# The rows of the large tiles in another order in DRAM: a grouped-query attention decode step with a gated MLP on one Trainium2 core

## The chip, the core and the metric

The kernel runs on one core of a Trainium2 chip. A core has five engines: TensorE (PE, with its weight loads, PEld), VectorE (DVE), ScalarE (ACT), GpSimd (POOL) and SyncE (SP), which here only issues transfers. Sixteen DMA engines move data between DRAM (HBM) and SBUF, the core's working memory of 128 partitions. The metric is the device time of one execution in microseconds; lower is better. Times of several executions are given as their median.

## The reference

One decode step for a batch of 8: a layer norm of x, attention over a cache of 4096 positions (32 query heads, 8 heads of K and V, head size 128), and a gMLP branch on x that gates the result. Everything is float32.

```python
def _A_ref(x, k_cache, v_cache, wq, wo):          # x is the layer-normed input, [8, 1, 512]
    q = (x @ wq).reshape(B, Sq, Hq, Dh).transpose(0, 2, 1, 3)
    k = jnp.repeat(k_cache, rep, axis=1)          # k_cache, v_cache: [8, 8, 4096, 128]
    v = jnp.repeat(v_cache, rep, axis=1)
    scores = jnp.einsum("bhqd,bhkd->bhqk", q, k) * (Dh ** -0.5)
    p = _softmax(scores, axis=-1)
    o = jnp.einsum("bhqk,bhkd->bhqd", p, v)
    return o.transpose(0, 2, 1, 3).reshape(B, Sq, Hq * Dh) @ wo

def _B_ref(x, w_in, w_sp, b_sp, w_out):
    z = _gelu(jnp.einsum("bsd,df->bsf", x, w_in))
    z1, z2 = z[..., :Fh], _layernorm(z[..., Fh:], axis=-1)
    g = jnp.einsum("ts,bsf->btf", w_sp, z2) + b_sp[None, :, None]
    return jnp.einsum("bsf,fd->bsd", z1 * g, w_out)

s = _A_ref(_layernorm(x), A_k_cache, A_v_cache, A_wq, A_wo)
g = _silu(_B_ref(x, B_w_in, B_w_sp, B_b_sp, B_w_out))
return x + s * g
```

Two things make up nearly all of the bytes: K and V, 134 MB each. Every byte of them is read once.

## The kernel before

SBUF holds three large buffers, the slots A, B and C, each 128 partitions of 16384 floats (64 KB a partition, 8 MB a slot). Everything large passes through them. `wq` goes to B and the weights of the MLP (`w_mlp`, 10496 floats a partition) to C; a small remainder of the MLP's output weights, `w_ext`, goes to the end of 32 partitions of C. Then for each of the eight K/V heads four loads follow: K for the first half of the batch to A (`load_k`, L591), K for the second half to B, V for the first half to C (`load_v`, L596), V for the second half to B again. At the end `wo` goes to A in seven pieces (`load_wo`, L601), of 14 down to 1 of its 32 blocks of 512 floats. In the last head the second half of V comes as two loads (L596 and L597).

All of these loads are issued by SP, one after the other, in the order in which they stand in the code. A load into a slot waits until PE has made the last matmul on what the slot held; the next load in SP's order cannot be issued before it. There are 42 loads of large tiles, one of `w_ext`, and the store of the result. The two loads of x are issued by ACT.

For a head, PE multiplies the query, spread over 32 columns, with K (L550, `scores`), DVE and ACT make the softmax, PE turns the probabilities round (L572) and multiplies them with V (L582, `values`), DVE picks and adds what belongs together (L584, L585), and PE folds the result (L588). The loop over heads is one on PE and DVE. A recording layer (`Recorder`) notes every operation with its reads and writes, derives the waits from them, and then writes the program out engine by engine; it does not reorder anything.

On the host, `kernel` lays every large array out so that DRAM holds the tile as it is to stand in SBUF: a row per partition, 128 rows for each load, and row p of DRAM goes to partition p. For K and V the arrays have the shape heads x 2 halves x 128 x 16384; `wq` and `wo` are 128 x 16384, `w_mlp` is 128 x 10496. A load of a slot thus reads 8 MB that lie in DRAM in one piece. For `wo` and for the split load of V a part of each row is read.

`w_ext` is the exception. In DRAM it has 8 groups of 4 rows and an unread fifth row, and the load reads groups and rows as two dimensions (L371).

Of the kernel before, what the change touches and what calls it, by code (L numbers as in the profile page):

```python
# [15 lines left out]
P = 128  # L16
B, D = 8, 512
# [23 lines left out]
XK = XG * XR  # L41
XC = P // XK
LAST = NB - 1


class Region:
# [300 lines left out]
def gqa_gmlp_decode(real, x, kT, v, wq, wo, w_mlp, w_ext, out):  # L347
    nc = Recorder(real)

    def sb(name, shape, **kw):  # L350
        return real.alloc_sbuf_tensor(name, shape, F32, **kw).ap()
# [4 lines left out]
    slots = {n: sb(f"slot_{n}", [P, SLOT], align_bytes=ALIGN) for n in "ABC"}  # L356
# [5 lines left out]
        nc.scalar.dma_start(xs_sb[:, c:c + XW // X_PARTS], x[:, c:c + XW // X_PARTS])  # L362
    x_sb = xs_sb[:, :D]

    nc.sync.dma_start(slots["B"], wq, key="B")
    wq_sb = slots["B"].rearrange("p (k n) -> p k n", k=NK)
    n_in, n_mlp = NK * 2 * FH, NK * 2 * FH + NB * D - XN
    nc.sync.dma_start(slots["C"][:, :n_mlp], w_mlp, key="C")
    w_in_sb = slots["C"][:, :n_in].rearrange("p (k n) -> p k n", k=NK)
    ext = slots["C"][:XK, n_mlp:n_mlp + XC * XN]  # L370
    nc.sync.dma_start(ext, w_ext[:, :XR])  # L371
# [59 lines left out]
    for i in range(E):  # L431
        for g in range(G):
            lo = g * P + i * W
# [23 lines left out]
    def mlp():  # L457
# [45 lines left out]
        nc.vector.tensor_copy(hT.rearrange("p a s -> p (a s)"), th)  # L503
        low = R * (LAST // 2)
        hX = tbuf[:XK, 2 * P + D:2 * P + D + XC * R].rearrange("p (c r) -> p c r", r=R)
        tx = scr[2][:XK, :XC * R].rearrange("p (c r) -> p c r", r=R)
        for c in range(XC):
            lo = (LAST % 2) * P + c * XK
            nc.tensor.transpose(tx[:, c, :], u[low:low + R, 1, lo:lo + XK], ident[low:low + R, low:low + R])
        nc.vector.tensor_copy(hX, tx)  # L510
        for j in range(NB):
            g = j % G
            w_j = w_out_sb(j)
            nc.tensor.matmul(sc[R * g:R * (g + 1), 0, :w_j.shape[1]], hT[:, j % 2, R * (j // 2):R * (j // 2 + 1)],
                             w_j, start=(j < G), stop=(j + G >= NB and j < LAST))
        g = LAST % G
        for c in range(XC):
# [70 lines left out]
        nc.tensor.matmul(po[:, b * REP:(b + 1) * REP], o_sb[b % 2], fold, start=True, stop=True)  # L588

    def load_k(h, half, n):  # L590
        nc.sync.dma_start(slots[n], kT[h, half], key=n)  # L591
        return slots[n].rearrange("p (i c g s) -> p i c g s", i=HALF, c=2, g=G)

    def load_v(h, half, n, own=0):
        cut = SLOT * (HALF - own) // HALF
        nc.sync.dma_start(slots[n][:, :cut], v[h, half][:, :cut], key=n)  # L596
        rest = nc.sync.dma_start(slots[n][:, cut:], v[h, half][:, cut:]) if own else None  # L597
        return slots[n].rearrange("p (i j e) -> p i j e", i=HALF, j=J), rest

    def load_wo(lo, hi):  # L600
        nc.sync.dma_start(slots["A"][:, lo * D:hi * D], wo[:, lo * D:hi * D])  # L601

    wo_sb = slots["A"].rearrange("p (m d) -> p m d", d=D)
    part, acc = sc[:, 0, :], sc[:, 1, :W]
# [16 lines left out]
    def head(h):  # L621
        spread_q(h)
        for half, n in enumerate("AB"):
            scores(half, load_k(h, half, n))
        softmax()
        for half, n in enumerate("CB"):
            v_sb, rest = load_v(h, half, n, 1 if h == HKV - 1 and half else 0)
            for i in range(HALF):
                b = half * HALF + i
                values(b, v_sb[:, i], rest if b == B - 3 else None)  # L630
                if b > 0:
                    combine(b - 1)
        combine(B - 1)
        if h < FOLDED // REP:
            to = oT[:, h]
        else:
            m = h * REP - FOLDED
            to = oT_end[:, m:m + REP, (E - 1) * B:E * B]
        nc.stored = nc.scalar.activation(to, po.rearrange("p (b r) -> p r b", r=REP), AF.Copy)
# [9 lines left out]
    for lo, hi in WO_PIECES:  # L649
        load_wo(lo, hi)  # L650
# [4 lines left out]
    for i in range(E):  # L655
        for g in range(G):
            lo = g * P + i * W
# [45 lines left out]
```

## Time and profile before

| | |
|---|---|
| time, median of 3 runs | 678.54 us (678.11 to 678.82) |
| span of the profiled execution, first to last instruction | 677.4 us |
| PE busy | 377.2 us (56%) |
| DVE busy | 165.3 us (24%) |
| ACT, POOL busy | 15.0 us (2%), 4.4 us (1%) |
| read from HBM, over the span | 290.74 MB, 429 GB/s |
| chain that ended last | DMA of wo 7%, PE L550 1%, the rest under 0.5% each |

The profile is of one execution. Its span runs from the first instruction to the last, and the time of an execution has a little more around it: the median lies 1.1 us above the span. The page gives busy time by engine, the span in 40 slices with the busy share in tenths, the share of the DMA engines and what they moved, and the chain of work that ended last, followed back from the last instruction. It reaches back only to the loads of wo, which were issued at 627 to 630 us and then waited behind earlier loads. For what comes before, the DMA rows of the slices have to be read, and SP's waits.

### The profile page before, as it was taken

The numbers are of one execution on the slowest core, as the hardware profiler recorded it, in microseconds if no ns is written. First come the engines' busy times: TensorE is split into PE (matmuls) and PEld (weight loads), VectorE is DVE, ScalarE is ACT, GpSimd is POOL, SyncE is SP. The second block draws the span as 40 slices with busy tenths as digits, with TensorE's granted clock in tenths as the row PEclk, the third lists the DMA queues.
The fourth block names the chain that finished last, engine by engine and source line by source line (L and its number), as shares of the span: only waits on it lengthen the run. The fifth ranks groups of instructions, "written<-read, shape, count | busy, mean of one in ns | idle before, by whom it ended". The sixth has DMA issues, their size and how long they took to land. (4 is left out here: it accounts for less than half of the span.)

```text
span 677.4 us, 6190 instructions
## 1 busy us (share of the span) xinstructions
PE 377.2 (56%) x2670; PEld 120.7 (18%) x2670; DVE 165.3 (24%) x262; ACT 15.0 (2%) x35; POOL 4.4 (1%) x22
## 2 busy tenths in 40 slices
PE   0638654546765464555755355656745356655576
PEld 0122121112211121111211021111211021111222
DVE  2051042301430033401521024400422024400442
ACT  0000000000000000000000000000000000000000
POOL 1000000000000000000000000000000000000000
PEclk9986767888776567878767678876667788876679
DMA  8999999999999999999999999999999999999997
GB/s 373 441 442 431 433 434 433 434 433 433 433 433 438 433 433 433 433 433 433 437 433 433 433 441 433 433 433 437 437 437 433 433 433 433 433 433 437 423 424 305
DMA packets 6270, 290.86 MB, mean 429 GB/s; under 512 B 840, under 2 KB 856, under 8 KB 1528
## 3 DMA queue, kind: packets, MB, share of 16 engines
q1 hardware_dynamic: 6232, 290.75, 99.2%
q8 instruction: 5, 0.08, 0.0%
q10 hardware_dynamic: 32, 0.02, 0.0%
q14 instruction: 1, 0.01, 0.0%
HBM read 290.74 MB, written 0.03 MB: 429 GB/s over the span
## 5 line engine op out<-in xcount | busy, mean ns | idle before, releaser
L550 PE MATMUL sc<-slot_B,qz 128*32 128x512 f32 x512 | 74.3, 745 | 77.9 <-PEq L550 77.9
L582 PE MATMUL o_ps<-slot_B,tbuf 128*16 128x512 f32 x512 | 76.9, 728 | 63.8 <-PEq L582 63.8
L550 PE MATMUL sc<-slot_A,qz 128*32 128x512 f32 x512 | 72.8, 733 | 44.9 <-PEq L550 44.9
L582 PE MATMUL o_ps<-slot_C,tbuf 128*16 128x512 f32 x512 | 76.8, 741 | 13.6 <-PEq L582 12.7
L584 DVE TENSOR_TENSOR o_all<-o_ps,diag 128x512 f32<-128x512 f32 x64 | 44.3, 691 | 137.4 <-DVEq L584 137.4
L554 DVE TENSOR_REDUCE nm<-sc 128x1 f32<-128x1024 f32 x8 | 9.8, 1224 | 273.9 <-DVEq L554 273.9
L585 DVE TENSOR_REDUCE o_sb<-o_all 128x128 f32<-128x512 f32 x64 | 67.7, 1059 | 9.3
L550 PEld LDWEIGHTS sc<-slot_B,qz 128*32 128x32 f32 x512 | 20.3, 133 | 131.8 <-issue 131.8
L550 PEld LDWEIGHTS sc<-slot_A,qz 128*32 128x32 f32 x512 | 20.0, 132 | 91.2 <-issue 91.2
L588 PE MATMUL po<-fold,o_sb 128*128 128x4 f32 x128 | 24.4, 261 | 18.2 <-PEq L588 16.7
L588 PEld LDWEIGHTS po<-fold,o_sb 128*128 128x128 f32 x128 | 20.1, 198 | 74.3 <-issue 74.3
L582 PEld LDWEIGHTS o_ps<-slot_B,tbuf 128*16 128x16 f32 x512 | 13.5, 106 | 92.7 <-issue 92.2
L582 PEld LDWEIGHTS o_ps<-slot_C,tbuf 128*16 128x16 f32 x512 | 15.6, 112 | 55.7 <-issue 55.4
L572 PE MATMUL scr<-ident,pbuf 128*128 128x128 f32 x64 | 15.5, 423 | 13.4 <-PEq L572 13.4
L555 ACT ACTIVATE pbuf<-sc,nm 128x1024 f32<-128x1024 f32 x8 | 8.9, 1114 | 281.3 <-DVEq L554 281.3
L572 PEld LDWEIGHTS scr<-ident,pbuf 128*128 128x128 f32 x64 | 12.6, 223 | 13.8 <-issue 13.8
L447 PE MATMUL scr<-slot_B,xnT 128*32 128x512 f32 x64 | 9.8, 764 | 8.1 <-PEq L447 8.1
L573 DVE COPY tbuf<-scr 128x512 f32<-128x512 f32 x16 | 11.1, 692 | 12.4 <-DVEq L573 12.4
L558 PE MATMUL scr<-ident,nm 128*1 128x128 f32 x8 | 2.2, 269 | 13.6 <-PEq L558 13.6
L565 PE MATMUL scr<-wl,same 128*128 128x1 f32 x16 | 3.6, 297 | 8.0 <-PEq L565 8.0
L426 PE MATMUL scr<-ident,tbuf 8*128 8x8 f32 x4 | 0.6, 255 | 12.9 <-DVE tbuf L423 12.9
L609 PE MATMUL sc<-slot_A,oT 128*8 128x512 f32 x48 | 6.5, 593 | 0.9 <-DMA slot_A<-in_wo 0.9
(105 smaller groups left out, 84.0 us busy)
## 6 DMA issues: line engine op xcount, KB each, us to landing
slot_B<-in_v SPq DMA_DIRECT2D x1, 6144.0 KB, 25.8
slot_C<-in_w_mlp SPq DMA_DIRECT2D x1, 5248.0 KB, 33.7
slot_A<-in_wo SPq DMA_DIRECT2D x1, 3584.0 KB, 36.8
slot_B<-in_v SPq DMA_DIRECT2D x1, 2048.0 KB, 28.7
slot_A<-in_wo SPq DMA_DIRECT2D x1, 2048.0 KB, 41.2
slot_A<-in_wo SPq DMA_DIRECT2D x2, 768.0 KB, 43.3
slot_A<-in_wo SPq DMA_DIRECT2D x1, 512.0 KB, 44.7
slot_A<-in_wo SPq DMA_DIRECT2D x2, 256.0 KB, 45.0
```

The costliest lines, as they stand in the source:

```text
L447: nc.tensor.matmul(pq[R * g:R * (g + 1), :], xnT[:, k, :], wq_sb[:, k, lo:lo + REP * DH], start=(k == 0), stop=(k == NK - 1))
L550: nc.tensor.matmul(sc[R * g:R * (g + 1), c, :], qz[:, b * R:(b + 1) * R], k_sb[:, i, c, g, :], start=(b == 0), stop=(b == B - 1))
L554: nc.vector.tensor_reduce(nm, sc, op=ALU.max, axis=AX.XY, negate=True)
L555: nc.scalar.activation(p.rearrange("p j s -> p (j s)"), sc.rearrange("p c s -> p (c s)"), AF.Exp, bias=nm, accum_out=l)
L565: nc.tensor.matmul(tot, same_all, wl, start=True, stop=True)
L572: nc.tensor.transpose(t[:, j * P:(j + 1) * P], p[:, 4 * c + j, :], ident)
L573: nc.vector.tensor_copy(pT[:, :, 4 * c:4 * c + 4].rearrange("p b j (g r) -> p (j g) b r", g=G), t.rearrange("p (m b r) -> p m b r", b=B, r ...
L582: nc.tensor.matmul(of[R * c:R * c + G * REP, :], pT[:, b, j, :], v_unit[:, j], start=(j < G), stop=(j >= J - G))
L584: nc.vector.tensor_mul(o_all[b % 2], o, diag[:, :, None].to_broadcast([P, G, DH]), after=after)
L585: nc.vector.tensor_reduce(o_sb[b % 2], o_all[b % 2].rearrange("p g d -> p d g"), op=ALU.add, axis=AX.X)
L588: nc.tensor.matmul(po[:, b * REP:(b + 1) * REP], o_sb[b % 2], fold, start=True, stop=True)
L609: nc.tensor.matmul(part[R * r:R * r + B, :], oT[:, h, r, :], wo_sb[:, m, :], start=(m < REP), stop=(m >= FOLDED - REP))
```

## The change

In DRAM the 128 rows of every large tile are put in another order. The 128 partitions are seen as 16 groups (e) of 8 partitions (j). Before, the row of partition 8 e + j was row 8 e + j. Now it is row 16 j + e: first the first partition of each of the 16 groups, then the second of each, and so on. The host puts the arrays into this order, and each load names its DRAM rows as two dimensions, e outside and j inside (`by_engine`), so that every partition gets the data that it had before. `w_ext`, x and the store of the result stay as they are.

```diff
 LAST = NB - 1
+QUEUES = 16
+
+
+def by_engine(rows):
+    return rows.rearrange("(j e) n -> e j n", e=QUEUES)
...
-    nc.sync.dma_start(slots["B"], wq, key="B")
+    nc.sync.dma_start(slots["B"], by_engine(wq), key="B")
...
-    nc.sync.dma_start(slots["C"][:, :n_mlp], w_mlp, key="C")
+    nc.sync.dma_start(slots["C"][:, :n_mlp], by_engine(w_mlp), key="C")
...
     def load_k(h, half, n):
-        nc.sync.dma_start(slots[n], kT[h, half], key=n)
+        nc.sync.dma_start(slots[n], by_engine(kT[h, half]), key=n)
...
     def load_v(h, half, n, own=0):
         cut = SLOT * (HALF - own) // HALF
-        nc.sync.dma_start(slots[n][:, :cut], v[h, half][:, :cut], key=n)
-        rest = nc.sync.dma_start(slots[n][:, cut:], v[h, half][:, cut:]) if own else None
+        nc.sync.dma_start(slots[n][:, :cut], by_engine(v[h, half][:, :cut]), key=n)
+        rest = nc.sync.dma_start(slots[n][:, cut:], by_engine(v[h, half][:, cut:])) if own else None
...
     def load_wo(lo, hi):
-        nc.sync.dma_start(slots["A"][:, lo * D:hi * D], wo[:, lo * D:hi * D])
+        nc.sync.dma_start(slots["A"][:, lo * D:hi * D], by_engine(wo[:, lo * D:hi * D]))
...
+    for name in ("kT", "v", "wq", "wo", "w_mlp"):
+        a = arrays[name]
+        rows = a.reshape(a.shape[:-2] + (QUEUES, P // QUEUES, a.shape[-1]))
+        arrays[name] = c(rows.swapaxes(-3, -2)).reshape(a.shape)
```

The instructions of every engine stand in the same order as before, with the same waits. SP's loads alone have another form. The first of them before, each with the partitions and floats that it writes:

```order
L365 DMA slot_B<-in_wq 128x16384
L368 DMA slot_C<-in_w_mlp 128x10496
L371 DMA slot_C<-in_w_ext 32x1x1024
L591 DMA slot_A<-in_kT 128x16384
L591 DMA slot_B<-in_kT 128x16384
L596 DMA slot_C<-in_v 128x16384
L596 DMA slot_B<-in_v 128x16384
```

And the same place in the changed kernel, whose lines stand five lower:

```order
L370 DMA slot_B<-in_wq 128x1x16384
L373 DMA slot_C<-in_w_mlp 128x1x10496
L376 DMA slot_C<-in_w_ext 32x1x1024
L596 DMA slot_A<-in_kT 128x1x16384
L596 DMA slot_B<-in_kT 128x1x16384
L601 DMA slot_C<-in_v 128x1x16384
L601 DMA slot_B<-in_v 128x1x16384
```

Nothing has moved. The loads of whole tiles have a third dimension on the side of SBUF, as only w_ext had; it answers to the two dimensions of rows, 16 x 8, that the DRAM side now has.

## The prediction

> **What bounds the kernel now.** I read the second and third part of the page first (engines and DMA in slices, DMA queues), then the chain that ended last, the table of stretches, and the waits of SP and PE.
>
> ```profile
> DMA  8999999999999999999999999999999999999997
> GB/s 373 441 442 431 433 434 433 434 433 433 433 433 438 433 433 433 433 433 433 437 433 433 433 441 433 433 433 437 437 437 433 433 433 433 433 433 437 423 424 305
> DMA packets 6270, 290.86 MB, mean 429 GB/s; under 512 B 840, under 2 KB 856, under 8 KB 1528
> q1 hardware_dynamic: 6232, 290.75, 99.2%
> ```
>
> The sixteen DMA engines are at nine tenths or more in all but the first and the last slice, and SP's queue, q1, takes 99.2% of their time. Slices hold a whole number of packets, so single ones read 431 or 441; the long stretches say it better:
>
> ```profile
> 40.00:340.00 300.00, 168.84 (x1113) 53.19 (x1110) 76.55 (x120) 7.11 (x17) 1.37 (x5) 0.74 1.00 433
> 340.00:640.00 300.00, 165.78 (x1094) 51.96 (x1098) 67.52 (x97) 6.42 (x16) 0.84 (x4) 0.74 1.00 434
> ```
>
> The columns are PE, PEld, DVE, ACT and POOL busy with their counts, the PE clock, the DMA share, GB/s. Over 600 us the DMA share is 1.00 and the rate 433 and 434; PE is busy for 56% of the same time. I take 433.5 GB/s, which is 27.1 GB/s for each of sixteen engines. A row of a slot is 16384 floats, 65536 B, so one engine takes 65536 B / 27.1 GB/s = **2.42 us a row**, and a load of 128 rows, eight to an engine, takes 19.4 us.
>
> ```profile
> 629.71 45.05 DMA slot_A<-in_wo
> 674.77 0.04 issue
> 674.81 0.47 PE sc L617 x16
> ```
>
> The chain ends with the landing of the last piece of wo at 629.71 + 45.05 = 674.8 us, and 2.6 us of matmuls, two DVE operations and the store lie behind it. Engines wait for loads, and loads wait for nothing: a time comes out as bytes over rate, plus both ends. 290.75 MB over 433.5 GB/s is 670.7 us; the span is 677.4, so 6.7 us lie outside the stream at full rate. The span is of one profiled execution; the median of the runs shown, 678.54, is 1.1 us above it, and I add that at the end.
>
> **The change: issuing.** No instruction is added, removed or moved. Every load of a large tile has a third dimension: the DRAM side counts 16 x 8 rows, the SBUF side 128 x 1. One load has had this form all along, w_ext at L371:
>
> ```profile
> 0.74 0.39 SPq L365 DMA_DIRECT2D slot_B<-in_wq  x1
> 1.18 0.41 SPq L368 DMA_DIRECT2D slot_C<-in_w_mlp  x1
> 1.64 0.82 SPq L371 DMA_DIRECT2D slot_C<-in_w_ext  x1
> 2.51 0.40 SPq L591 DMA_DIRECT2D slot_A<-in_kT  x1
> ```
>
> It held SP for 0.82 us, its neighbours of two dimensions for 0.39 to 0.41. So I give each changed issue 0.82 - 0.40 = 0.42 us more; the bounds are 0 (the third dimension costs nothing, and w_ext's 32 partitions did) and 0.43 (0.82 - 0.39). Only the first of them is in the open: nothing streams before wq is issued. That is **+0.4 us**. Behind it each of the other 41 changed issues is covered by loads that are queued already:
>
> ```profile
> L591 SPq DMA_DIRECT2D slot_B<-in_kT x8: 327/327/328, 33.9 to 588.1; - x8
> DMA to landing us min/median/max: 26.9/44.5/53.1
> DMA to landing us min/median/max: 25.8/33.7/47.3
> ```
>
> The first two lines are L591's (kT), the third is L596's (v). The shortest time from issue to landing of a kT load is 26.9 us, and its own 19.4 us of rows leave 7.5 us in which the engines still worked on what was ahead of it. The shortest of v, 25.8 us, is that of the 6 MB load, which streams for 14.5 us: 11.3 us of cover. An issue that takes 0.82 us instead of 0.33 uses 0.5 us of this. If the cover were gone, 41 x 0.42 = 17 us would be in the open.
>
> **The change: where the engines are.** The bytes, the row length and the number of rows per engine stay, so a load that the engines do undisturbed takes 19.4 us as before. What changes is which rows, and so which partitions, are under way at the same moment. I take it that with an outer dimension of sixteen one engine takes one index of it, hence eight neighbouring partitions: engine 0 writes partitions 0 to 7 in this order, engine 1 writes 8 to 15, and so on, so that at any moment the partitions written lie eight apart. How rows were shared out before is not in the trace, and no row of it shows engines that get in each other's way in SBUF. So I bound it. **Lower end:** the order of partitions costs nothing, each row stays at 2.42 us, and +0.4 us remains. **Below nothing:** reading neighbours could be quicker than reading distant rows. The load of w_mlp answers to that, whose rows are 41984 B long and so lie at another distance than those of K and V. Between 22.6 and 34.1 us it is alone:
>
> ```profile
> GB/s 0 0 292 1898 146 0 0 0 1314 1022 0 0 0 584 1752 0 0 0 146 1752 438 0 0 0 1022 1314 0 0 0 438 1752 146 0 0 0 1314 1022 0 0 0
> DMA packets 112, 4.70 MB, mean 409 GB/s; under 512 B 0, under 2 KB 0, under 8 KB 0
> ```
>
> Bytes are counted where a row begins. The 40 columns are 0.29 us each; seven bunches of sixteen rows begin about 5.4 columns or 1.56 us apart, and 41984 B in 1.56 us is 27.0 GB/s an engine, the 27.1 of K and V. The distance between rows leaves no mark on the rate, which looks set by the engines. What distant rows could cost is then at most in the first slice, where 373 stands against 433.5: (1 - 373/433.5) x 16.9 us = 2.4 us. Of that 1.1 us pass until the first issue ends; I allow 1 us of gain. **Upper end:** engines meet in pairs on one way into SBUF, so two rows take the time of two, one after the other: 2 x 2.42 = 4.84 us a row. More than two to a way I leave out, as sixteen engines over 128 partitions in equal strides give no reason for it.
>
> Between these ends no row of a trace decides, since all rows shown here are of the old sharing. The nearest thing to the new one is w_ext, which had its groups of four partitions each on an engine of its own; its bytes are too few to tell a rate. I take the upper end because the new order makes the same kind of meeting in every load, in step: all engines start together and all rows are equally long.
>
> [...]
>
> **The sum.** In pairs, and in step but for what one engine started ahead of the other. All sixteen are started by one issue of 0.39 us, so a pair is at most 0.39 us apart, 0.16 of a row. Two engines that go through four rows on one way and four on the next share it for 4 - d rows and are alone for d, so four rows take (8 - d) row times: with d = 0.16, 7.84 in place of 4, a factor of 1.96. Stream 670.7 x 1.96 = 1314.6; outside it 6.7; first issue 0.4; execution against median 1.1. **Together 1323 us.** The compute has room: PE's 377 us of work lie in a stream twice as long, and a later landing only makes SP's cover longer.
>
> ```profile
> SPq L591 <- PEq L582: 274.1, 7, 40.3
> SPq L596 <- PEq L550: 245.9, 7, 37.6
> PE 377.2 (56%) x2670; PEld 120.7 (18%) x2670; DVE 165.3 (24%) x262; ACT 15.0 (2%) x35; POOL 4.4 (1%) x22
> ```
>
> SP waits up to 40.3 us for PE to give a slot back. These waits look like a bound and are not one, since loads ahead are still streaming; with loads of 38 us they change their length only.
>
> **The rivals.**
>
> *Nothing meets.* Either the hardware deals partitions out as before whatever the DRAM side looks like, or one way takes two engines at full rate. Then rows stay at 2.42 us, the first issue costs 0 to 0.43 us, and the time is 678.5 to 679.0: no slower than can be told. That is the case on the other side. It decides as soon as either condition holds, for all loads at once. For it speaks that w_ext in the third dimension went by without a mark in the rate of its slice (442, the third); against it that a form with 16 outside and 8 inside leaves each engine hardly another choice than eight neighbouring partitions.
>
> [...]
>
> *Neighbours are quicker.* By the rows at most the 1 us at the start, less 0.4: 677.9 us. The change then does what it says and there is little to win, because the rate in between is flat. Only if w_mlp's rate were no measure could the stream gain as well.
>
> *The change does not do what it says* is contained in the first: if engines do not take one outer index each, rows read together are not neighbours, and nothing else changes either.
>
> **How the numbers follow.** In step and in pairs 0.40, own range 1200 to 1350 (d up to one row, factor 1.75, gives 1182; no lead at all 1350). Out of step 0.20, 726 to 1200. Nothing meets 0.36, around 678.9. Neighbours quicker 0.04, half of it by more than 0.2%. A measurement of this kernel tells 0.2%, 1.4 us, from no change. Slower by more is 0.40 + 0.20 + 0.02 (an issue that costs more than w_ext shows) = 0.62; within it 0.34 + 0.02 = 0.36; faster 0.02. The range must keep the third case as well as the first, so it goes from 678.2 to 1350; no narrower one leaves out two in ten only.
>
> **What would show it.** Issuing: SP's rows at L370, L596 and L601 of the changed kernel at about 0.8 us instead of 0.33 to 0.44. Meeting: GB/s near 220 in all slices with the DMA share still at 1.00, since engines that share a way are busy all the time; PE's busy share near 28%; the landing of a kT load at 38 us or more after its issue. [...] Nothing meets: 433 in all slices and a span of 677 to 678. One thing would make the prediction wrong: that the way into SBUF is not shared as I take it. Then the 643.9 us of it (1314.6 - 670.7) go and 0.4 stays.

## The result, and the profile after

| | before | after |
|---|---|---|
| time, median of 4 runs | 678.56 us (678.11 to 678.82) | 1402.51 us (1394.30 to 1403.58) |
| span of the profiled execution | 677.4 us | 1402.2 us |
| PE busy, of the span | 56% | 27% |
| read from HBM, over the span | 429 GB/s | 207 GB/s |

The changed kernel takes 2.064 times the time of the kernel before (95% interval 2.061 to 2.067, from all runs together; the two medians alone give 2.067). The direction of the forecast held. The time did not: 1402.5 us lie above the 1323 forecast and above the upper end of the range, 1350.

From the page of the changed kernel come the row of the engines, the two DMA rows of the 40 slices, and the row of SP's queue:

```profile
PE 383.0 (27%) x2670; PEld 122.5 (9%) x2670; DVE 165.2 (12%) x262; ACT 15.0 (1%) x35; POOL 4.4 (0%) x22
...
DMA  9999999999999999999999999999999999999998
GB/s 210 217 197 206 210 197 209 209 209 209 209 210 209 209 208 209 206 209 208 208 202 209 208 209 198 209 209 209 209 209 209 209 209 209 209 208 206 201 209 196
...
q1 hardware_dynamic: 6232, 290.75, 99.8%
```

The engines' work is what it was (PE 383.0 us against 377.2). SP's queue has the same 6232 packets and the same 290.75 MB. SP's queue takes 99.8% of the DMA engines' time where it took 99.2%, and they move half as much, 207 GB/s against 429, evenly from the first slice to the last. So a busy share near one says that an engine has a packet in hand, not how fast it moves it. Two long stretches have the numbers (columns as in the prediction):

```profile
120.00:720.00 600.00, 152.90 (x1018) 47.96 (x1010) 66.92 (x96) 6.22 (x15) 0.63 (x3) 0.62 1.00 208
720.00:1280.00 560.00, 146.95 (x986) 45.50 (x978) 62.46 (x86) 5.01 (x13) 0.84 (x4) 0.62 1.00 208
```

208 GB/s is 13.0 GB/s an engine, against 27.1. How long a row takes is seen when 20.5 us of the changed kernel are cut into 40 columns of 0.51 us, with the bytes counted where a row begins:

```profile
GB/s 895 0 671 128 0 384 0 0 0 0 895 128 512 128 128 256 0 0 0 0 895 128 512 128 256 128 0 0 0 384 512 128 512 128 256 128 0 0 0 384
```

All sixteen rows of a bunch begin within some three microseconds, then nothing begins, and the next bunch follows ten columns or 5.1 us later. The packet records of the whole trace agree: of the 4096 rows of 64 KB the median is 5.106 us and the mean 5.055, where the kernel before has 2.418. No row takes less than 4.48 us. Those rows alone are 4096 / 16 x 5.055 = 1294 us for each engine, 92% of the span.

The chain of waits ends as before, with the last piece of wo, only that the profile no longer finds its queue's name:

```profile
1399.56 0.01 another core or an unknown queue
1399.57 0.04 issue
1399.61 0.47 PE sc L622 x16
```

The piece is issued at 1296.8 us and lands some 103 us later, at 1399.6; 2.6 us lie behind it, as many as before.

SP's issues in the order of time, then the groups of the kT load at L596 and of the v load at L601 with what their loads took to land:

```profile
0.74 0.67 SPq L370 DMA_DIRECT2D slot_B<-in_wq  x1
1.47 0.57 SPq L373 DMA_DIRECT2D slot_C<-in_w_mlp  x1
2.08 0.79 SPq L376 DMA_DIRECT2D slot_C<-in_w_ext  x1
```

```profile
L596 SPq DMA_DIRECT2D slot_A<-in_kT x8: 572/600/600, 2.9 to 1132.0; - x8
L596 SPq DMA_DIRECT2D slot_B<-in_kT x8: 536/536/537, 54.6 to 1214.1; - x8
DMA to landing us min/median/max: 69.0/103.6/111.7
```

```profile
DMA to landing us min/median/max: 63.3/85.9/110.0
```

The changed form costs 0.28 us in the first issue (0.67 - 0.39) and about 0.2 in the others (0.54 to 0.60 against 0.33 to 0.44), not 0.42. One issue stands apart on both sides: the last piece of wo held SP for 13.4 us before and holds it for 41.9 us now, with earlier loads still streaming. A kT load lands 69.0 us or more after its issue, v 63.3 or more. SP still waits for PE to give slots back, now for up to 81.7 us at a time:

```profile
SPq L596 <- PEq L587: 567.5, 7, 81.7
SPq L601 <- PEq L555: 536.9, 7, 78.8
```

As before, these waits bound nothing: loads ahead of them are streaming.

### The profile page after: what moved, and what is told of

Its sections match the earlier page's. It is cut to its first block, busy times and chain, and to the rows that moved or that the text cites. A ratio compares the mean times of both kernels' runs of the same rounds, so it can differ in the third digit from the quotient of the medians.

```text
span 1402.2 us, 6190 instructions
## 1 busy us (share of the span) xinstructions
PE 383.0 (27%) x2670; PEld 122.5 (9%) x2670; DVE 165.2 (12%) x262; ACT 15.0 (1%) x35; POOL 4.4 (0%) x22
## 3 DMA queue, kind: packets, MB, share of 16 engines
q1 hardware_dynamic: 6232, 290.75, 99.8%
## 5 line engine op out<-in xcount | busy, mean ns | idle before, releaser
L589 DVE TENSOR_TENSOR o_all<-o_ps,diag 128x512 f32<-128x512 f32 x64 | 44.2, 691 | 475.7 <-DVEq L589 471.9
L577 PE MATMUL scr<-ident,pbuf 128*128 128x128 f32 x64 | 15.5, 423 | 13.4 <-PEq L577 13.4
L614 PE MATMUL sc<-slot_A,oT 128*8 128x512 f32 x48 | 11.3, 1005 | 12.3 <-DMA slot_A<-in_wo 12.3
L474 PE MATMUL scr<-slot_C,xnT 128*32 128x256 f32 (+1 forms) x64 | 6.0, 516 | 14.2 <-PEq L474 14.2
L573 DVE TENSOR_SCALAR pbuf<-pbuf,w 128x1024 f32<-128x1024 f32 x8 | 6.0, 752 | 1.2 <-DVEq L573 0.2
## 6 DMA issues: line engine op xcount, KB each, us to landing
slot_B<-in_v SPq DMA_DIRECT2D x1, 6144.0 KB, 63.3
```

Of the source, the lines that this page charges most:

```text
L474: nc.tensor.matmul(pz[R * g:R * (g + 1), part * FQ:part * FQ + n], xnT[:, k, :], w_in_sb[:, k, part * FH + lo:part * FH + lo + n], start=( ...
L577: nc.tensor.transpose(t[:, j * P:(j + 1) * P], p[:, 4 * c + j, :], ident)
L589: nc.vector.tensor_mul(o_all[b % 2], o, diag[:, :, None].to_broadcast([P, G, DH]), after=after)
L614: nc.tensor.matmul(part[R * r:R * r + B, :], oT[:, h, r, :], wo_sb[:, m, :], start=(m < REP), stop=(m >= FOLDED - REP))
```

## The experiments

My theory after the result was: which partitions an engine serves has changed, engines meet in pairs on one way into SBUF, and the order of the rows in DRAM has nothing to do with it. The rivals: neighbouring rows read together are themselves slow in DRAM; the third dimension is slow; the extra 5% over two rows' time have a cause of their own. Way, pair and meeting are words of the theory, and so are the engines e and e + 4 and the four neighbouring partitions that the expectations speak of: no trace shows a way into SBUF or names the engine of a packet. No experiment leaves computation out. The kernel before took 678.56 to 678.82 us beside them. The time of each is one execution. Four executions of the changed kernel lie between 1394.30 and 1403.58 us, so a few microseconds between two experiments say nothing; the verdicts rest on rates and row times of the traces.

**The same dealing, DRAM as before.** `e1_far` keeps the 16 x 8 form, but group e reads rows that lie one behind the other, as they did before. A spare row that is not read follows each group of eight, so that the two dimensions stay apart.

```diff
-    return rows.rearrange("(j e) n -> e j n", e=QUEUES)
+    return rows.rearrange("(e j) n -> e j n", e=QUEUES)[:, :P // QUEUES]
...
-        arrays[name] = c(rows.swapaxes(-3, -2)).reshape(a.shape)
+        rows = np.concatenate([rows, np.zeros_like(rows[..., :1, :])], axis=-2)
+        arrays[name] = c(rows).reshape(a.shape[:-2] + (-1, a.shape[-1]))
```

> The loads keep the third dimension and 16 groups of 8 rows, but in DRAM the rows lie as before: group e holds the rows of partitions 8e to 8e+7 one behind the other, with one spare row behind each group that is not read. Rows read at the same time are far apart again. Theory (engines meet in pairs on the way into SBUF because of the dealing of partitions): about 1402 us, as the changed kernel, if meeting alone makes a 64 KB row take 5.1 us; about 1330 us if meeting costs exactly a factor of two and the remaining 5% come from neighbouring rows. Rival (neighbouring rows in DRAM are slow to read): about 679 us.

It took 1397.53 us. Its slices:

```profile
GB/s 211 212 199 207 211 201 210 210 210 210 207 211 208 208 208 208 208 205 210 208 210 207 207 208 210 210 210 210 210 210 207 210 207 210 210 207 210 202 211 201
```

Distant rows, 209 GB/s in the long stretches where the changed kernel has 208, a median row of 5.09 us, and a time within the spread of the changed kernel. Neither the loss nor its extra 5% come from the place of the rows in DRAM.

**Neighbours in DRAM, the old dealing.** `e2_near` is the other half: 128 partitions stay the outer dimension, as before the change, and the rows of K, V and wq are cut into pieces of 8 KB, with the pieces of all partitions side by side in DRAM. The loads have a third dimension here too.

```diff
+PIECE = 2048
...
+def pieces(rows):
+    return rows.rearrange("c p n -> p c n")
...
-        nc.sync.dma_start(slots[n], kT[h, half], key=n)
+        nc.sync.dma_start(cut_up(slots[n]), pieces(kT[h, half]), key=n)
```

> Neighbours in DRAM without another dealing: every row of K, V and wq is cut into 8 pieces of 8 KB, and in DRAM the pieces with one number of all 128 partitions lie together, so the sixteen engines read within 1 MB all the time. The outer dimension is 128 as in the kernel before; wo and the MLP's weights stay as they were. Theory (dealing of partitions): near the kernel before, 678 us and some 15 us more, as 8 times as many packets each carry the 9 ns that a packet of 64 KB shows above its bytes (6 KB pieces of wo: 234 ns for 226 ns of bytes): 690 to 697 us. Rival (neighbours in DRAM): about 1400 us. Rival (third dimension as such): about 1400 us.

The 9 ns are an estimate from packets of the kernel before: 65536 B take 2418 ns and 6144 B 234, which gives 27.19 GB/s and some 8 ns beside it. The run took 687.34 us, less of a loss than expected. Two long stretches of it:

```profile
40.00:340.00 300.00, 167.23 (x1110) 52.64 (x1106) 73.67 (x117) 7.11 (x17) 1.36 (x5) 0.76 1.01 428
340.00:640.00 300.00, 160.68 (x1076) 49.63 (x1068) 68.10 (x98) 6.42 (x16) 0.84 (x4) 0.76 1.01 428
```

428 GB/s: neighbours and a third dimension do no harm, and no good either. The 1.3% of time fit the cutting: a piece takes 309 ns by the median, so that eight take 8 x 0.309 = 2.47 us where a row took 2.42. That is 2% more; the rate shows only 1.2% of it, and the DMA share of 1.01 says that the pieces of an engine overlap a little.

**The plain form, but half the partitions at a time.** In `e3_halves` nothing of the change is left but the suspect: each load becomes two plain loads of 64 partitions (the 2 MB rest of V stays one).

```diff
+PARTS = [(0, 64), (64, P)]
...
-        nc.sync.dma_start(slots[n], kT[h, half], key=n)
+        for lo, hi in PARTS:
+            nc.sync.dma_start(slots[n][lo:hi], kT[h, half][lo:hi], key=f"{n}{lo}")
```

> The kernel before with its DRAM order and its plain form of two dimensions, but each load of a large tile is issued as two, partitions 0 to 63 and 64 to 127 (the 2 MB piece of V in the last head stays one load). Theory (two engines on one way into SBUF): 64 partitions reach only half of the ways, so sixteen engines share them in pairs: about 1400 us, or some 20 us more, since here no pair is ever out of step (5.1 us for every 64 KB row). Rivals (neighbours in DRAM, third dimension): about 680 us, as neither is there.

1403.82 us, to 0.1% the time of the changed kernel:

```profile
GB/s 210 211 199 206 202 208 209 209 209 209 209 208 207 207 206 207 207 204 209 209 202 207 207 209 209 209 209 209 209 209 206 209 207 206 207 206 206 206 218 195
```

The DRAM order and the plain form are those of the kernel before; what differs is that a load covers 64 partitions, and so which partitions are served at the same time. That the loads are smaller is not it: in the kernel before, the 49152 B rows of V's 6 MB load take 1.815 us and the 28672 B rows of the first piece of wo 1.062 us, 27.1 and 27.0 GB/s an engine, with 128 partitions each. So the cause lies in which partitions are served at the same time; why these take longer together, no run shows.

**Shifting engines against each other, three misses in a row.** If the loss comes from engines in step, keeping them apart in time should bring speed back. Extra loads at the start by GpSimd, long and short ones in turn, were to delay some engines more than others. `e4_step` wrote them into slot A, `e5_apart` into the unused end of slot C; `e6_both`, the control, had its long and short ones in pairs.

```diff
+    spare = slots["C"][:, 11520:]
+    for i, long in enumerate((1, 0, 1, 0) * 4):
+        lo, hi = (0, 4096) if long else (4096, 4112)
+        p0 = 16 * (i // 2)
+        nc.gpsimd.dma_start(spare[p0:p0 + 16, lo:hi], by_engine(kT[0, 0])[:4, :4, lo:hi])
```

> The changed kernel, with two extra loads of 1 MB at the start, issued by GpSimd into slot A before its first real load. Each runs on four engines only, four rows an engine; two loads of 64 B rows stand between and behind them so that they should fall on engines 0 to 3 and 8 to 11 (or 4 to 7 and 12 to 15). From then on those engines are four rows behind. Theory (engines e and e + 4 meet while in step): out of step by four rows they hardly meet, and all later loads run near 433 GB/s: 720 to 780 us, the slices' rate above 380 GB/s after the first 20 us. If GpSimd's loads fall on other engines, only some pairs part and the time stays at 1402 to 1420 us, since the slowest pair sets it. Rivals (neighbours in DRAM, third dimension): 1410 us.

> The changed kernel with 16 small extra loads at the start, issued by GpSimd into a part of slot C that nothing reads. Eight of them bring 256 KB to four engines (64 KB to each), eight bring 1 KB; long and short take turns, so that the long ones fall on every other group of four engines, and these start the stream 256 KB, four rows, behind the others. Unlike in e4_step, no load of SP waits for them. Theory (engines e and e + 4 meet while in step): the pairs are parted, and the rate goes to near 433 GB/s until a lead is lost: 720 to 790 us. Rival (meeting does not depend on step, or other engines meet): 1395 to 1420 us.

> The control to e5_apart: the same 16 extra loads, with the same bytes, in the order long, long, short, short, so that both engines of a pair e, e + 4 start the stream late, and the other pairs start early. Theory (engines e and e + 4 meet): all pairs stay in step, 1400 to 1425 us. Rival (any engines four rows apart are helped, or the extra loads themselves do it): as e5_apart.

They took 1400.48, 1406.32 and 1427.58 us, the last 2.6 us above its range. All three had a fault that the trace shows: SP's next load into the same part of the slot had to wait for the extra loads, until 79.9 us in `e4_step`, 154.3 in `e5_apart` and 172.6 in `e6_both`. The queues ran short of work (DMA share 0.44, 0.66 and 0.37 in the 10 to 24 us before), and all engines came together again: the sixteen landings of the load behind the wait lie only 1.4 to 2.4 us apart. The slices of `e5_apart`:

```profile
GB/s 210 215 216 241 178 208 207 209 207 209 209 209 209 209 209 209 209 209 209 209 209 209 209 209 207 209 209 209 209 209 209 209 209 209 209 205 209 194 214 197
```

The fourth slice reaches 241, the fifth falls to 178, and from then on nothing is left of the shift. A hint, no more.

**Sixteen partitions at a time.** In `e7_four` the K loads come as eight loads of 16 partitions; all else is as before the change. That four neighbouring partitions are one way is an assumption of the expectation.

```diff
+PARTS = [(p, p + 16) for p in range(0, P, 16)]
...
-        nc.sync.dma_start(slots[n], kT[h, half], key=n)
+        for lo, hi in PARTS:
+            nc.sync.dma_start(slots[n][lo:hi], kT[h, half][lo:hi], key=f"{n}{lo}")
```

> The kernel before, with each load of K (134 of the 291 MB) issued as eight loads of 16 partitions, so that each engine writes one partition a load and four engines write four neighbouring partitions at once. Theory (four partitions are one way, and engines on it share it): a 64 KB row takes four times as long. Without any loss from sharing, 9.67 us a row and 16 x 8 x (9.67 - 2.42) = 928 us more: 1607 us; with the 5.6% loss that two engines showed (5.1 us for a pair's rows), 10.2 us a row and 998 us more: 1677 us; more, if the loss grows with the number of engines. Rival (only the spacing of eight partitions hurts): about 680 us.

1520.21 us, below both numbers. K and V can be told apart in the slices of the page; below them 40 us in the first K phase in 40 columns, and the stretch around it:

```profile
GB/s 394 111 110 111 136 411 110 110 110 112 428 110 119 112 116 430 102 124 114 138 408 114 121 129 219 328 120 133 138 375 180 148 150 287 269 129 119 133 364 287
```

```profile
GB/s 0 262 131 328 197 131 0 0 0 0 131 262 197 328 131 0 0 0 0 0 393 66 393 197 0 0 0 0 0 393 0 393 131 131 0 0 0 0 197 197
```

```profile
60.00:110.00 50.00, 0.00 (x0) 0.00 (x0) 0.67 (x2) 0.00 (x0) 0.00 (x0) 0.50 1.03 115
```

While K streams, the rate of the long stretches is 109 to 115 GB/s up to 350 us; while V streams, whose loads are whole, 394 to 430. Bunches begin some 9.3 us apart, and the packet records have 9.28 us as the row of this phase. That is about a quarter of the rate, as the assumption had it, though nothing in the trace shows four engines together. And the row takes 4% *less* than four rows' time, 4 x 2.418 = 9.67 us, where in the changed kernel it takes 5.6% more than two: 4 x 65536 B / 9.28 us = 28.2 GB/s for four rows, 2 x 65536 B / 5.106 us = 25.7 for two. With 9.28 us a row the expectation's sum gives 1557 us. The rest goes with the later K phases, whose slices read mostly 112 to 150 where 110 stood: the sixteen landings of a K load lie 3.5 us apart in the first phase and 14 to 26 us from 640 us on, so engines fall out of step.

**Shifting engines, mended.** `e8_apart` lets the extra loads copy from DRAM to DRAM, 2 MB in all, and nothing but the end of the program waits for them. GpSimd's loads of four outer groups go to four engines each, it seems (in `e8_apart` twelve landings of wq come at 43.6 to 44.2 us, four at 49.6 to 50.1), so that long, short, long, short shifts four engines against the four that they meet by the theory. The control `e9_both` (long, long, short, short) shifts eight engines alike.

```diff
+    spare = real.dram_tensor("spare", (4 * 16, SLOT), F32, kind="Internal").ap()
+    for i, long in enumerate((1, 0, 1, 0)):
+        n = SLOT if long else 16
+        nc.gpsimd.dma_start(spare[16 * i:16 * i + 16, :n], by_engine(kT[0, 0])[:4, :4, :n])
```

> e5_apart without its flaw (SP's load of V into slot C waited 68 us for the extra loads, the queues ran dry and all engines were together again): four extra loads at the start, issued by GpSimd, from DRAM to a spare place in DRAM; long (four rows of 64 KB on each of four engines), short, long, short. Only the end of the program waits for them. Theory (engines e and e + 4 meet while in step; apart they stay apart): 720 to 800 us, slices near 430 GB/s after some 100 us. If leads do not last although no queue runs dry, 1000 to 1405 us, with a rate that falls back to 209 GB/s. Rival (step does not matter): 1395 to 1415 us with 209 GB/s throughout.

> The control to e8_apart: the same four extra loads in the order long, long, short, short, so that both engines of a pair e, e + 4 are late in one half of the engines and neither is in the other. Theory: no pair is parted, 209 GB/s throughout, 1400 to 1425 us. Rival (any delay of some engines helps): as e8_apart.

1211.02 and 1408.68 us. Long stretches, the first three of `e8_apart`, the others of `e9_both`:

```profile
100.00:200.00 100.00, 32.09 (x210) 10.28 (x210) 11.50 (x18) 1.41 (x3) 0.00 (x0) 0.64 1.00 245
300.00:700.00 400.00, 126.13 (x803) 38.04 (x805) 52.16 (x70) 3.41 (x9) 0.63 (x3) 0.62 1.00 243
700.00:1100.00 400.00, 126.26 (x832) 39.52 (x824) 55.52 (x78) 4.82 (x12) 0.63 (x3) 0.64 1.00 244
```

```profile
100.00:200.00 100.00, 22.85 (x164) 7.94 (x162) 6.39 (x15) 1.66 (x4) 0.00 (x0) 0.62 1.01 209
300.00:700.00 400.00, 107.73 (x714) 34.17 (x714) 48.39 (x70) 4.62 (x11) 0.42 (x2) 0.62 1.01 209
```

The same extra bytes and nearly the same delays, in another order: one gains 14% on the changed kernel, the other nothing. In `e9_both` the sixteen landings of a load lie mostly 9 to 12 us apart, in two groups of eight, so engines are far out of step there too, and nothing is gained. In `e8_apart` they lie 6.5 us apart in the first load, 11.9 in the second and some 19 to 28 from the fifth on. So it matters which engines are out of step with which. The theory's pairs fit both runs, but the traces name no engine and so do not show them. And most of the way back is missing: 244 of 433 GB/s, and the 726 us of the forecast's lower end for out of step are not reached. By 300 us slot B's next load is issued only 2 to 4 us before the first engine is through with the load before it, which leaves the leaders little to run ahead on. Whether that is what stops them was not tried, and the DMA share of 1.00 in these stretches speaks against it, as it shows no engine without work.

**Where the extra 5% come from: two more misses.** I supposed that a pair loses time by the distance between the partitions that its two engines write; the 32 of the expectation is an assumption. `e10_quarters`, built as `e3_halves` with loads of 32 partitions, was to make this distance small. `e11_eight` is `e1_far` with eight groups of sixteen, so that eight engines work, in four pairs by the theory.

```diff
-PARTS = [(0, 64), (64, P)]
+PARTS = [(p, p + 32) for p in range(0, P, 32)]
```

```diff
-QUEUES = 16
+QUEUES = 8
```

> As e3_halves, with every load of a large tile issued as four of 32 partitions (the 2 MB piece of V stays one). [...] Theory (the 5% beyond a factor of two come from changing between partitions 32 apart on one way): 218 GB/s and 1335 to 1350 us. Rival (they come from two engines sharing as such): 209 GB/s and 1400 us, or up to 20 us more.

> [...] Theory (the 5% beyond a factor of two belong to each pair by itself): a 64 KB row takes 5.1 us again, half of e1_far's rate (104 GB/s) and twice its time, about 2790 us. Rival (they come from sixteen engines streaming at once): 4.84 us a row and about 2660 us.

`e10_quarters` took 1405.51 us, with a median row of 5.118 us and 207 to 208 GB/s in the long stretches. Loads of 32 partitions in place of 64 bring nothing; that theory fell. `e11_eight` took 2420.55 us, well below both expectations, and its rate climbs:

```profile
20.00:300.00 280.00, 41.40 (x312) 14.20 (x312) 13.20 (x36) 0.89 (x2) 0.73 (x2) 0.68 0.50 109
300.00:500.00 200.00, 24.96 (x156) 8.54 (x156) 17.72 (x26) 1.61 (x4) 0.21 (x1) 0.55 0.50 112
500.00:1000.00 500.00, 75.71 (x494) 23.84 (x494) 29.90 (x44) 3.02 (x7) 0.21 (x1) 0.56 0.50 120
1000.00:1500.00 500.00, 75.21 (x498) 23.69 (x498) 29.89 (x44) 3.21 (x8) 0.42 (x2) 0.57 0.50 124
```

The DMA share of 0.50 shows that only eight engines ever work. In the first 200 us two rows in three take 4.98 to 5.06 us, 3 to 5% over the 4.84 us of two rows, and the eight landings of the first load lie within 1 us. From 800 us on half of the rows take 4.82 to 4.83 us and the others less, down to 2.67, and the landings of a load lie some 36 us apart. So at the start eight engines in step lose nearly as much a row as sixteen, which speaks against a loss that needs all sixteen; then they fall out of step by themselves, and the surplus over two rows' time is gone as well. Why it goes, and what the 5.6% come from, was not settled.

## Why the prediction was right in its direction and wrong in its time

- **Bound by the stream:** right. The queue's share is 99.8%, and the time is bytes over rate plus the ends.
- **Issuing:** over-sized and without weight. 0.82 us of w_ext was taken for every third dimension; measured are 0.54 to 0.67. The first one costs 0.28 us where 0.4 was forecast, and the other 41 stay hidden, as forecast: the shortest time from issue to landing is now 63.3 us.
- **Which end applies:** the upper, and a little beyond it. That the partitions served at the same time set the rate is shown by `e3_halves` (208 GB/s with no other part of the change in it), and that step has a part in it by `e8_apart` (243 to 245 GB/s) against its control `e9_both` (207 to 209). "Engines meet in pairs on one way into SBUF" was an assumption that gave nearly the right factor; no run shows the way or the pairs. Nearest before was the argument that the form 16 x 8 leaves engines hardly another choice than eight neighbours. That each engine does take one outer index stays an inference, since the packets of the trace don't name their engine; the DMA share of 0.50 with eight outer indices in `e11_eight` agrees with it, and so do the 32 packets of `w_ext` before, which form eight chains of four, each packet some 0.155 us behind the last.
- **The failed step:** "so two rows take the time of two, one after the other: 2 x 2.42 = 4.84 us a row". It took that a shared way is shared without loss, and the own range ended at 1350, the same term with no lead. Measured is a median row of 5.106 us, 5.6% more. No row of the trace before could give this; the fault was to treat the worked-out value as an upper end, when sharing could also cost.
- **In step:** right; "d = 0.16" is over-sized. No run shows the sum's term "four rows on one way and four on the next"; what the packets show are rows of 5.055 us on average against the median of 5.106. If the median is a row shared from end to end, four rows save 4 x 0.051 = 0.20 us, or 0.08 of a row of 2.42 us. The rate stays flat at 208 GB/s over 1160 us.
- **The sum:** the span was to be 1323 - 1.1 = 1321.9 us and is 1402.2, 80 us more. With d = 0.08 the factor is 7.92 / 4 = 1.98 instead of 1.96, 13 us; the issue gives back 0.1; the other 67 us, 5% of a stream of 1328, are by difference what a row takes beyond the time of two.
- **Neighbours quicker:** rightly given little. w_mlp's rate was a good witness: distant rows ran at 209 GB/s in `e1_far` where neighbours had 208, and the neighbouring pieces of `e2_near` at 428 where the kernel before had 433.
- **Fewer partitions in a load:** loads of 64, 32 and 16 partitions run at a half, a half and a quarter of the rate (208, 207 to 208, and 109 to 115 GB/s against 433). The long stretches of the changed kernel, `e1_far`, `e3_halves`, `e9_both` and `e10_quarters` show 207 to 209 GB/s, short of half of 433.5, 216.8.
- **Out of step:** possible, but not by itself in this kernel. It took an outside shove (`e8_apart`), and its 1211.02 us lie just above the 726 to 1200 of the forecast. No run shows what the 726 would need, a lead at which no engine holds another up; shown are 243 to 245 GB/s with the landings of a load up to 28 us apart.

## What to carry to other kernels

In this kernel, whose loads stream at the rate of all sixteen DMA engines, the partitions that are served at the same time mattered and the order of the rows in DRAM did not. So keep 128 partitions as the outermost dimension of a full load, on both sides, and put any rearranging into inner dimensions, as `e2_near` did at 428 GB/s and a cost of 1.3%. Loads of 16 to 64 partitions ran at a quarter to a half of the rate here. A DMA share of 1.00 with half the GB/s (208 of 433) was the mark of it, and when such a halving is forecast, its end of the range should leave room for a loss on top, here 5.6% a row.

## What the runs showed of the hardware that was not expected

- A row of 64 KB does not take just two or four times its 2.418 us of before: 5.106 us in the changed kernel (2.11 times), 5.03 with eight engines in step and 4.82 once they are out of step (2.08 and 1.99 times, `e11_eight`), 9.28 with loads of 16 partitions (3.84 times, `e7_four`). Why is open.
- Engines keep step for the whole run in the changed kernel, where the sixteen landings of a load never lie more than 2.6 us apart, and partly lose it in `e7_four` (26 us) and `e11_eight` (36 us).
- The issue of a load took longer or shorter by its form: 0.33 to 0.44 us for plain rows, 0.54 to 0.67 with 16 x 8, 0.79 to 0.82 with the 8 x 4 of `w_ext`. The last piece of wo is an exception (13.4 us before, 41.9 after), and in `e2_near` some issues held SP for up to 6.3 us, though their form took 0.37 to 0.44 us where nothing held them.
